# Cosine attention and an x·cos(x) MLP in one kernel: one pipeline over units of six heads instead of two phases

## The chip, the cores and the metric

The kernel runs on one core of one Trainium2 chip. The metric is device time in microseconds (us). Each kernel runs several times, always beside runs of the kernel before on the same chip. The runs were made on more than one chip, so kernels are best compared by their ratios. In these kernels TensorE does the matmuls and transposes, VectorE elementwise work and reductions, ScalarE activations and copies, GpSimd (POOL in the profile) further elementwise work, and SyncE (SP) issues DMA transfers. SBUF is the core's on-chip memory; the rows of a tensor in it are called partitions (64x448 lies on 64 of them). "Unit" means six heads of one batch (16 units), "pair" two heads, and a "step" is a quarter of a pair's scores (12 steps per unit).

## The reference

```python
# q, k, v: (8 batches, 12 heads, 448 tokens, 64); tau = 0.1
q_n = q / (norm(q) + 1e-6);  k_n = k / (norm(k) + 1e-6)
attn = softmax(q_n @ k_n.T / tau)
x = (attn @ v) as (3584 tokens, 768)
h = x @ w_in                    # 768 x 2048
out = (h * cos(h)) @ w_out      # 2048 x 768
```

## The kernel before

It has two blocks, one after the other. The first does attention head by head and writes `xT`; the second does the MLP over tiles of 512 tokens. V is padded with 64 columns of ones, so the product of the exponentials and V holds the softmax sums already repeated on 64 partitions. VectorE takes a reciprocal of all of them, for each of the 96 heads:

```python
def norm(g):                                   # VectorE, once per head
    vec.wait_ge(s_av, g + 1)
    vec.reciprocal(rtmp[gp].ap()[D:2*D, :], AV[gp].ap()[D:2*D, :])   # 64 x 448
    ...
    vec.tensor_tensor(xt_dst, AV[gp].ap()[0:D, :], rtmp[gp].ap()[D:2*D, :], ALU.mult)

for g in range(NG):                            # TensorE
    emit_av(g)                                 # 4 matmuls, 128 columns of V|ones
    if g + 1 < NG: emit_sc(g + 1)              # 4 matmuls, 64 rows each
    if g + 3 < NG: emit_tp(g + 3)              # 8 transposes
# ... a second block: m1 (x @ w_in), Sin on ScalarE, product on VectorE, m2 (@ w_out)
```

## Time and profile before

| | before |
|---|---|
| median time | 841.01 us (840.73 to 841.48, 3 runs) |
| attention | 0 to 522 us |
| MLP | 522 to 838 us |

First, the costliest groups on the page of the kernel before. The columns are: line, engine, operation, tiles, shapes and count; then busy time in us and the mean ns of one; then the engine's idle time just before them and who ended it.

```profile
L237 DVE RECIPROCAL rtmp<-AV 64x448 f32<-64x448 f32 x96 | 284.2, 2960 | 44.1 <-PE AV L352 39.8
L337 PE MATMUL SCP<-qkT_sb 64*112 64x448 bf16 x384 | 166.8, 587 | 56.3 <-DVE qkT_sb L228 54.2
L425 PE MATMUL PH<-xT,W 128*128 128x512 bf16 x672 | 156.5, 383 | 14.7 <-DVE gT L486 10.8
L440 PE MATMUL PO<-W,gT 128*128 128x384 bf16 x896 | 146.6, 326 | 0.0
```

Second, the table of windows of the kernel before: stretch, its length, then busy us (instructions) of TensorE, its weight loads, VectorE, ScalarE and GpSimd, then the granted clock, the DMA share and GB/s. One window lies in attention, one in the MLP.

```profile
200.00:300.00 100.00, 81.67 (x312) 35.37 (x310) 90.68 (x66) 59.33 (x69) 25.52 (x12) 1.00 0.29 72
571.00:592.00 21.00, 21.00 (x130) 12.62 (x129) 0.69 (x1) 3.12 (x4) 0.00 (x0) 1.00 0.19 57
```

In attention VectorE is busy for 91% of the time, and the reciprocal is most of that. In the second window TensorE does almost nothing but second-layer matmuls (128 of 130), one per 0.162 us.

Third, the timeline of TensorE in attention (start us, length us, then the instructions). The weight load of each next score matmul starts with that matmul:

```profile
300.46 1.74 PE L337 MATMUL SCP<-qkT_sb 64*112 64x448 bf16 x4
300.88 0.21 PEld L337 LDWEIGHTS SCP<-qkT_sb 64*112 64x112 bf16 x1 [0.16 <-issue]
301.25 0.21 PEld L337 LDWEIGHTS SCP<-qkT_sb 64*112 64x112 bf16 x1 [0.16 <-issue]
```

The 448 columns take 0.37 us, 1.2 columns per ns, while 384 columns in the MLP take 0.162 us, 2.4 per ns. In the kernel after, whose clock records cover such stretches, first-layer matmuls of 448 columns lie 0.373 us apart at a granted clock of 0.50 and 0.189 us at 1.00 (medians); "half clock" and "full clock" below mean these two rates. In the MLP's first 3.4 us here the matmuls of 512 columns lie 0.427 us apart, and 0.216 us from 525.5 us on. What brings full clock this trace does not show: attention kept TensorE busy for 82% (200 to 300 us) and stayed at half clock to its end, while the MLP, whose waits for VectorE are at most 0.3 us, stayed at full clock from 525.5 us on. The clock column says 1.00 in attention too, only because the trace's first clock record is that of 525.5 us.

### The profile page before, as it was taken

To read this page: it belongs to the slowest core of one execution; us is meant where nothing else is said; L and a number is where in the kernel's file an instruction comes from. 1 tells how busy PE (TensorE), PEld (TensorE's weight loads), DVE (VectorE), ACT (ScalarE), POOL (GpSimd) and SP (SyncE) were. 2 spreads that over 40 slices of the span, in tenths; PEclk is the share of its full clock that TensorE was granted. 3 is DMA by queue.
4 is the path that set the end of the run, shared out by engine and by line. 5 is a ranking of instruction groups with operands and counts; after the bars stand their busy time and mean duration, and the time that the engine had idled before them with its cause. 6 is when DMAs were issued, how large, how long until landed. Compare 5 with 4: busy or idle time off the path is not lost. (4 is left out here: it accounts for less than half of the span.)

```text
span 838.7 us, 7918 instructions
## 1 busy us (share of the span) xinstructions
PE 706.1 (84%) x3104; PEld 321.0 (38%) x3104; DVE 535.0 (64%) x438; ACT 407.3 (49%) x494; POOL 132.1 (16%) x60
## 2 busy tenths in 40 slices
PE   0797797797797797797797797999999999999997
PEld 0343243243243243243333342335454444445464
DVE  3698898898898898898898898441312223131400
ACT  4656656656656656756755733442323333232311
POOL 3434124124113113213213200000000000000000
PEclk9999999999999999999999999999999999999999
DMA  9761452364033043034040000001111020102022
GB/s 286 209 198 61 115 174 80 94 174 89 10 100 99 1 98 97 3 98 98 2 99 0 1 0 1 1 0 39 38 37 39 20 56 20 57 1 76 0 76 76
DMA packets 40516, 57.13 MB, mean 68 GB/s; under 512 B 1824, under 2 KB 34080, under 8 KB 39712
## 3 DMA queue, kind: packets, MB, share of 16 engines
q1 hardware_dynamic: 40480, 56.63, 24.5%
q8 instruction: 25, 0.41, 0.2%
q14 instruction: 11, 0.09, 0.0%
HBM read 45.61 MB, written 11.01 MB: 68 GB/s over the span
## 5 line engine op out<-in xcount | busy, mean ns | idle before, releaser
L237 DVE RECIPROCAL rtmp<-AV 64x448 f32<-64x448 f32 x96 | 284.2, 2960 | 44.1 <-PE AV L352 39.8
L290 ACT ACTIVATE expT<-SCP 112x896 bf16<-112x896 f32 x192 | 165.4, 913 | 165.4 <-PE SCP L337 165.4
L337 PE MATMUL SCP<-qkT_sb 64*112 64x448 bf16 x384 | 166.8, 587 | 56.3 <-DVE qkT_sb L228 54.2
L486 DVE TENSOR_TENSOR gT<-PH,cosh 128x512 bf16<-128x512 f32 x112 | 77.5, 692 | 194.7 <-ACT cosh L459 194.7
L352 PE MATMUL AV<-expT,vp 112*128 112x448 bf16 x384 | 160.5, 572 | 35.4 <-ACT expT L290 34.3
L425 PE MATMUL PH<-xT,W 128*128 128x512 bf16 x672 | 156.5, 383 | 14.7 <-DVE gT L486 10.8
L440 PE MATMUL PO<-W,gT 128*128 128x384 bf16 x896 | 146.6, 326 | 0.0
L337 PEld LDWEIGHTS SCP<-qkT_sb 64*112 64x112 bf16 x384 | 65.7, 200 | 161.1 <-DVE qkT_sb L228 118.6
L459 ACT ACTIVATE cosh<-PH,cst 128x512 f32<-128x512 f32 x112 | 77.0, 688 | 88.3 <-PE PH L425 88.3
L440 PEld LDWEIGHTS PO<-W,gT 128*128 128x128 bf16 x896 | 87.7, 98 | 58.6
L425 PEld LDWEIGHTS PH<-xT,W 128*128 128x128 bf16 x672 | 58.2, 98 | 112.0 <-DVE gT L486 51.0
L177 POOL TENSOR_TENSOR kb<-Kf,rk 112x1536 bf16<-112x1536 f32 x16 | 44.2, 2762 | 340.9 <-ACT rk L281 340.9
L468 ACT ACTIVATE out_sb<-PO 128x768 f32<-128x768 f32 x28 | 22.7, 811 | 123.6 <-PE PO L440 123.6
L352 PEld LDWEIGHTS AV<-expT,vp 112*128 112x128 bf16 x384 | 38.4, 126 | 97.6 <-issue 55.2
L319 PE MATMUL TP<-ident,qs 112*64 112x112 bf16 x384 | 55.7, 301 | 21.7 <-POOL qs L180 21.6
L319 PEld LDWEIGHTS TP<-ident,qs 112*64 112x64 bf16 x384 | 35.3, 158 | 83.6 <-issue 83.6
L228 DVE COPY qkT_sb<-TP 64x896 bf16<-64x896 bf16 x96 | 58.7, 612 | 12.7 <-PE TP L323 11.1
L241 DVE TENSOR_TENSOR xT<-AV,rtmp 64x448 bf16<-64x448 f32 x96 | 59.3, 618 | 3.3
L323 PE MATMUL TP<-ident,kb 112*64 112x112 bf16 x384 | 55.8, 301 | 0.0
L180 POOL TENSOR_TENSOR qs<-Qf,rq 112x1536 bf16<-112x1536 f32 x16 | 44.2, 2762 | 0.0
L323 PEld LDWEIGHTS TP<-ident,kb 112*64 112x64 bf16 x384 | 43.9, 177 | 0.0
L273 ACT ACT_TABLE_LOAD x16 | 20.5, 1283 | 37.8 <-DVE qn L215 37.8
(25 smaller groups left out, 233.5 us busy)
## 6 DMA issues: line engine op xcount, KB each, us to landing
Qf<-in_q_dram SPq DMA_DIRECT2D x16, 672.0 KB, 5.5
Kf<-in_k_dram SPq DMA_DIRECT2D x16, 672.0 KB, 8.5
Vf<-in_v_dram SPq DMA_DIRECT2D x16, 672.0 KB, 9.9
wstage<-in_moe_w_in_dram SPq DMA_DIRECT2D x6, 1024.0 KB, 8.3
wstage<-in_moe_w_out_dram SPq DMA_DIRECT2D x4, 1536.0 KB, 6.7
out_dram<-out_sb SPq DMA_DIRECT2D x8, 336.0 KB, 2.6
out_dram<-out_sb SPq DMA_DIRECT2D x8, 288.0 KB, 2.6
out_dram<-out_sb SPq DMA_DIRECT2D x8, 240.0 KB, 2.5
```

Of the source, the lines that this page charges most:

```text
L228: vec.tensor_copy(qkT_sb[gp].ap(), TP[gp].ap()).then_inc(s_ev, 1)
L237: vec.reciprocal(rtmp[gp].ap()[D : 2 * D, :], AV[gp].ap()[D : 2 * D, :]).then_inc(s_vself, 1)
L241: vec.tensor_tensor(xt_dst, AV[gp].ap()[0:D, :], rtmp[gp].ap()[D : 2 * D, :], ALU.mult).then_inc(s_dv, 1)
L290: act.activation(dst, src, ACT.Exp).then_inc(s_exp, 1)
L319: last = pe.transpose(TP[gp].ap()[0:D, NP * j : NP * (j + 1)], qs[i].ap()[:, col : col + D], ident.ap())
L323: last = pe.transpose(TP[gp].ap()[0:D, S + NP * j : S + NP * (j + 1)], kb[i].ap()[:, col : col + D], ident.ap())
L337: ins = pe.matmul(outap, lhsT, rhs, start=True, stop=True)
L352: ins = pe.matmul(AV[gp].ap(), lhsT, rhs, start=(j == 0), stop=(j == NJ - 1))
L425: ins = pe.matmul(PH[t % 2].ap(), W1v[:, c, 128 * nb : 128 * nb + 128], xTv[:, c, MB * sb : MB * sb + MB], start=(c == 0), stop=(c == NKC ...
L440: ins = pe.matmul(PO[T2 % 2].ap()[:, 512 * n2h : 512 * n2h + N2W], gTv[sbp % 2][:, f, 128 * ms : 128 * ms + 128], W2v[:, f, N2W * n2h : N2 ...
L459: act.activation(cosh[t % 2].ap(), PH[t % 2].ap(), ACT.Sin, bias=cst.ap()[:, 1:2], scale=1.0).then_inc(s_cos, 1)
L486: vec.tensor_tensor(gTv[sb % 2][:, nb, :], PH[t % 2].ap(), cosh[t % 2].ap(), ALU.mult).then_inc(s_gm, 1)
```

## The change

The new kernel keeps one pipeline. Its aims are to get the 96 reciprocals off VectorE, to run the scores of two heads side by side in the two halves of the array, and to fill TensorE's gaps in attention with matmuls of the second MLP layer of earlier batches.

- V gets one column of ones, not 64, so the sums of a head are one row (partition 64 of `xu`).
- Small transfers (`sums`, one per pair) gather the rows of six heads on partitions 0 to 5. One reciprocal (6 x 448) serves six heads. Six transfers, below called the broadcast, then repeat each head's row on 64 partitions (`RB`), and VectorE multiplies.
- First-layer blocks follow every second unit; second-layer matmuls are spread over the steps of units 3 to 15 (`m2_fill`).

The core of the diff, cut (`...`):

```diff
-    vec.reciprocal(rtmp[gp].ap()[D : 2 * D, :], AV[gp].ap()[D : 2 * D, :])      # x96
-    vec.tensor_tensor(xt_dst, AV[gp].ap()[0:D, :], rtmp[gp].ap()[D : 2 * D, :], ALU.mult)
+    def av_tail(g): ...
+        P.op("ACT", lambda e: e.activation(xuv[i][:, 2*p : 2*p+2, :], AVv[0 : D+1, :, 0:S], ACT.Copy, bias=0.0), ...)
+        P.op("SP", lambda e: e.dma_start(sums[i].ap()[2*p : 2*p+2, :], xuv[i][D : D+1, 2*p : 2*p+2, :]), ...)
+    def recip(u):
+        P.op("DVE", lambda e: e.reciprocal(rcp[i].ap(), sums[i].ap()), ...)       # 6 x 448, x16
+        for h in range(UH):
+            o = P.op("SP", lambda e, h=h: e.dma_start(RBv[:, h, :],
+                     bass.AP(rcp[i], h * S, [[S, 1], [0, D], [1, S]])), ...)      # one row to 64 partitions
+    def normalise(u, a):
+        P.op("DVE", lambda e: e.tensor_tensor(xTv[b % 2][...], xuv[i][0:D, a::2, :], RBv[:, a::2, :], ALU.mult), ...)
...
+    def unit(u, per_quantum):
+        for kq in range(4 * UP):              # 12 steps
+            scores(g, c)                      # two heads, rows 0-63 and 64-127 of the array
...
+            if kq == 6 and u >= 1:  recip(u - 1)
+            if kq >= 10 and u >= 1: normalise(u - 1, kq - 10)
+            if per_quantum: m2_fill(per_quantum[kq % len(per_quantum)])
...
+            if c == 3 and g + 1 < NG: transposes(g + 1)
...
+        if u >= 2 and u % 2 == 0:
+            m1(u // 2 - 1)
```

## The prediction

> **What bounds the kernel now.** It has two phases in series. The table of windows puts attention at 0 to 522 us and the MLP at 522 to 838 us. In attention VectorE is busy 0.91 (200 to 300 us): per head a reciprocal of 2.96 us, a copy of 0.61 and a multiply of 0.62, so 4.19 us x 96 heads = 402 us, plus reductions. TensorE hides under it, but barely, because it runs at half speed: by the timeline, starts of its 448-column matmuls lie 0.37 us apart[...]; in the MLP 512 columns take 0.216 us from 525.5 us on. The clock row shows 1.0 throughout. [...]the MLP's first 3.4 us have 0.427 us per matmul. The MLP is TensorE-bound: 672 x 0.216 + 896 x 0.1625 = 291 us.
>
> **What the change does.**
> - Reciprocals: 96 x 2.96 = 284 us become 16 of the same length (448 elements on 6 partitions): 47 us.
> - The sums become one row: AV has 65 columns, its copy goes to ScalarE (48 x 0.91 us).
> - The second layer (896 matmuls) is spread over units 3 to 15, the first layer stays in eight dense blocks. The bound moves to TensorE.
>
> **New load of TensorE, full clock.** First layer 768 x 0.189 = 145 us; second 146; score pairs 48 x 4 x 0.19 = 36 if the two row tiles run together (I assume so; no trace shows it); AV 48 x 7 x 0.19 = 64; transposes 48 x 7 x 0.056 = 19. Sum 410 us.
> VectorE about 275 us and ScalarE about 300 us (192 x 0.8 exps, 64 x 1.0 sines, 48 x 0.9 copies, rest) fit below.
>
> **Lost time on TensorE's chain (estimates from this trace).**
> - Switches between row-tiled and full matmuls: 0.13 us now between scores and transposes; 27 per unit, about 0.12 each: 3.2 us a unit.
> - The transposes of a pair are followed at once by its scores: copy 0.61 plus two latencies, 1.1 us, 3 per unit.
> - Units 0 to 2 have no second-layer work and should run at half clock as attention does now: about 22 us each.
>
> Sum: start 14; units 0 to 2, 66; units 3 to 15, 7 x 21.7 + 6 x 24.3 = 298; eight first-layer blocks 145; their entries and exits 8 x 3 = 24; tail (last normalisation, 144 second-layer matmuls, store) 32. **About 580 us, range 500 to 680.** Chances: faster 0.97, same 0.02, slower 0.01.
>
> **What would show each step.**
> - Second-layer matmuls 0.1625 us apart in units 3 to 15; the chain mostly TensorE; units of 22 to 24 us.
> - Paired scores starting within some 10 ns of one another; 0.19 us apart would add 36 us.
> - "PE scores waits for DVE qkT copy", 48 times, about 1 us each.
>
> **What would make it wrong.** The largest risk is the clock: if the half speed returns in units 3 to 15 (their matmuls fill only some 65% of the time), each unit costs up to 12 us more, and the time is 650 to 720 us. If switches cost nothing and copies hide, 500 us. VectorE's order (reciprocal of 2.96 us or a reduction in front of the copy of the transposes) could lengthen each pair's gap by 1 to 2 us, 50 to 100 us in all.

That units 3 to 15 would run at full clock was an estimate of mine.

## The result, and the profile after

| | before | after |
|---|---|---|
| median time | 840.87 us (4 runs) | 927.19 us (925.85 to 927.68, 4 runs) |
| ratio | | 1.1027 (95%: 1.1011 to 1.1042): slower |
| TensorE busy | 706.1 us | 503.7 us |
| VectorE busy | 535.0 us | 276.8 us |
| mean granted clock | (not recorded in attention) | 0.797 |

A ratio is the mean time of one kernel's runs over that of the other's of the same rounds, so it is not quite the ratio of the medians.

The busy times fell as meant and no engine is near full, yet the time rose. The page of the kernel after, busy time and share of the span by engine:

```profile
PE 503.7 (54%) x2768; PEld 237.4 (26%) x2768; DVE 276.8 (30%) x268; ACT 288.4 (31%) x358; POOL 189.9 (21%) x160
```

The chain that ended last, by engine and then by line, names what the time is made of:

```profile
PE 33%; DMA 26%; SPq 21%; DVE 14%; ACT 2%; issue 2%; POOL 2%; ACTq 0%
DMA RB<-rcp 24%; SPq L379 19%; PE SC L401 12%; PE PO L446 8%; PE AV L401 6%; DVE rcp L376 5%; DVE xT L386 5%; PE AV L357 2%; PE SC L339 2%; DMA sums<-xu 2%; PE SC L446 1%; DVE qkT L326 1%; DVE osb L454 1%; ACT xu L369 1%; SPq L262 1%
```

The transfers that repeat the reciprocals (`RB<-rcp`) and their issue (line 379) are 43% of the chain. Groups and DMA issues of the page, the latter with KB each and us from issue to landing:

```profile
L376 DVE RECIPROCAL rcp<-sums 6x448 f32<-6x448 f32 x16 | 47.0, 2936 | 20.5 <-DMA sums<-xu 20.5
L386 DVE TENSOR_TENSOR xT<-xu,RB 64x1344 bf16<-64x1344 f32 x32 | 49.6, 1551 | 350.6 <-DMA RB<-rcp 350.4
RB<-rcp SPq DMA_DIRECT2D x96, 112.0 KB, 13.6
```

The reciprocals cost 47 us, as predicted. VectorE then stands idle for 350 us, in front of the multiply that needs `RB`. The list of waits (who waited for what; us in total, times, longest) shows how this goes on to TensorE:

```profile
DVE xT L386 <- DMA RB<-rcp: 350.4, 16, 24.4
PE SC L339 <- DVE qkT L326: 199.6, 40, 23.0
PE SC L401 <- DVE xT L386: 98.1, 5, 24.0
PE AV L401 <- DVE xT L386: 65.1, 3, 28.1
```

In this trace VectorE took its instructions in the order of the program. Behind the blocked multiply stands the copy of the next pair's transposes (`qkT`): in the timeline below the transposes run at 332.16 us, and their copy starts at 351.90 us, after the multiply, which waited until 348.28 us. So TensorE waits for that copy at the end of half of the units, and for `xT` itself in front of the eight first-layer blocks. The timeline of the kernel after around one such wait, where the brackets hold the engine's idle time and what ended it:

```profile
320.55 2.93 DVE L376 RECIPROCAL rcp<-sums 6x448 f32<-6x448 f32 x1
323.51 15.16 SPq L379 DMA_DIRECT2D RB<-rcp  x6
332.16 0.55 PE L323 MATMUL TP<-ident,qks 128*128 128x128 bf16 x7
338.71 6.76 SPq L371 DMA_DIRECT2D sums<-xu  x2
348.28 3.12 DVE L386 TENSOR_TENSOR xT<-xu,RB 64x1344 bf16<-64x1344 f32 x2 [21.05 <-DMA RB<-rcp]
351.54 0.90 PE L401 MATMUL SC<-xT,W 128*128 128x448 bf16 x2 [18.83 <-DVE xT L386]
351.90 0.62 DVE L326 COPY qkT<-TP 128x896 bf16<-128x896 bf16 x1
```

From the end of the reciprocal (323.5 us) to the multiply (348.3 us) pass 24.8 us, and this is so in all 16 units (24.7 to 25.6 us). Even the issue of the six transfers takes 15 us. The sums of later heads, which go through the same queue, are issued after them.

In the trace's packet records, a packet of 1792 bytes (one row) from `rcp` takes 0.93 us in the median; packets of 1536 bytes of other transfers take 0.13 us. The records of one unit come in rounds of 16, one round each 1.054 us: 16 x 1792 B / 1.054 us = 27.2 GB/s. The 64 packets of one transfer, about 16 in flight at a time, all read one row. My guess, which no trace had shown and which the experiments test, is that the place they read limits the rate. (The word "ports" in two names of runs comes from that guess.)

### The profile page after: what moved, and what is told of

Same layout as the page of the kernel before. It is cut to its first block, busy times and chain, and to the rows that moved or that the text cites. A ratio compares the mean times of both kernels' runs of the same rounds, so it can differ in the third digit from the quotient of the medians. Undisturbed runs are those within 1.5% of the kernel's fastest.

```text
span 924.9 us, 6907 instructions
## 1 busy us (share of the span) xinstructions
PE 503.7 (54%) x2768; PEld 237.4 (26%) x2768; DVE 276.8 (30%) x268; ACT 288.4 (31%) x358; POOL 189.9 (21%) x160
## 4 chain that ended last, share of the span: by engine, by line
PE 33%; DMA 26%; SPq 21%; DVE 14%; ACT 2%; issue 2%; POOL 2%; ACTq 0%
DMA RB<-rcp 24%; SPq L379 19%; PE SC L401 12%; PE PO L446 8%; PE AV L401 6%; DVE rcp L376 5%; DVE xT L386 5%; PE AV L357 2%; PE SC L339 2%; DMA sums<-xu 2%; PE SC L446 1%; DVE qkT L326 1%; DVE osb L454 1%; ACT xu L369 1%; SPq L262 1%
## 5 line engine op out<-in xcount | busy, mean ns | idle before, releaser
L347 ACT ACTIVATE PX<-SC 128x896 bf16<-128x896 f32 x144 | 130.4, 915 | 273.4 <-PE SC L339 271.9
L339 PE MATMUL SC<-qkT 64*128 64x448 bf16 x288 | 56.6, 398 | 212.9 <-DVE qkT L326 199.6
L290 POOL TENSOR_TENSOR sq<-raw 128x896 bf16<-128x896 f32 x47 | 78.2, 1681 | 444.5 <-DVE n L291 433.3
L401 PE MATMUL SC<-xT,W 128*128 128x448 bf16 x516 | 111.9, 377 | 98.1 <-DVE xT L386 98.1
L386 DVE TENSOR_TENSOR xT<-xu,RB 64x1344 bf16<-64x1344 f32 x32 | 49.6, 1551 | 350.6 <-DMA RB<-rcp 350.4
L307 POOL TENSOR_TENSOR qks<-raw,rn 128x896 bf16<-128x896 f32 x47 | 79.3, 1687 | 113.1 <-ACT rn L301 113.1
L401 PE MATMUL AV<-xT,W 128*128 128x448 bf16 x252 | 57.7, 384 | 65.1 <-DVE xT L386 65.1
L401 PEld LDWEIGHTS SC<-xT,W 128*128 128x128 bf16 x516 | 53.0, 103 | 153.1 <-issue 112.1
L357 PE MATMUL AV<-PX,va 128*65 128x448 bf16 x288 | 76.9, 380 | 0.0
L291 DVE TENSOR_REDUCE n<-sq 128x14 f32<-128x896 bf16 x48 | 50.8, 1081 | 36.0 <-POOL sq L290 32.0
L376 DVE RECIPROCAL rcp<-sums 6x448 f32<-6x448 f32 x16 | 47.0, 2936 | 20.5 <-DMA sums<-xu 20.5
L326 DVE COPY qkT<-TP 128x896 bf16<-128x896 bf16 x48 | 29.6, 616 | 29.3 <-PE TP L323 29.3
```

The source lines that it names most:

```text
L290: P.op("POOL", lambda e: e.tensor_tensor(sq[j].ap(), src, src, ALU.mult), [("raw", i, p)], [("sq", j)])
L307: P.op(eng, lambda e: e.tensor_tensor(qksv[i][:, :, h, :].rearrange("p s h d -> p h s d"), rawv[i][:, h, :, :], bass.AP(rn[i], p * 2 * NS, ...
L339: P.op("PE", lambda e, r=r, a=a, rhs=rhs: e.matmul(sc[:, a, 0:S], qkT[j].ap()[r, S + TL + 128 * c : S + TL + 128 * c + 128], rhs, start=Tr ...
L347: P.op("ACT", lambda e: e.activation(PXm[j][:, c], sc[:, :, 0:S], ACT.Exp, scale=1.0 / TAU), ["SC%d" % z], [("PX", j, c)])
L357: P.op("PE", lambda e, c=c: e.matmul(AVv[0 : D + 1, a, 0:S], vav[i][:, 8 * p + 4 * a + c, :], PXm[j][:, c, a, :], start=(c == 0), stop=False),
L376: P.op("DVE", lambda e: e.reciprocal(rcp[i].ap(), sums[i].ap()), [("sums", i, p) for p in range(UP)], [("rcp", i)])
```

## The experiments

The theories: **A**, the place in SBUF that all packets of the broadcast read limits it, and its time goes through VectorE's order to TensorE. **B**, the six issues or the number of packets limit it, wherever they read. **C**, the half clock (mean 0.797) is the loss, and the waits are not. All ratios are to the kernel before in the same rounds. The diffs are shortened: bookkeeping and the calls after the last unit are left out.

### x1_ports: the same broadcast from eight rows, four partitions apart

The `sums` transfers now write eight copies of a head's row, four partitions apart; the reciprocal runs on 64 partitions (2.94 us, as before); each broadcast reads all eight copies.

```diff
-    sums = sbs("sums", 2, [UH, S], F32);  rcp = sbs("rcp", 2, [UH, S], F32)
+    NR, NCP, CST = 64, 8, 4;  HP = [0, 1, 2, 3, 32, 33]
+    sums = sbs("sums", 2, [NR, S], F32);  rcp = sbs("rcp", 2, [NR, S], F32)      # set to 1.0 once
-    dma_start(sums[i].ap()[2*p : 2*p+2, :], xuv[i][D : D+1, 2*p : 2*p+2, :])
+    for h in (2*p, 2*p + 1):
+        dma_start(bass.AP(sums[i], HP[h]*S, [[CST*S, NCP], [1, S]]),
+                  bass.AP(xu[i], D*UH*S + h*S, [[UH*S, 1], [0, NCP], [1, S]]))
-    bass.AP(rcp[i], h * S, [[S, 1], [0, D], [1, S]])
+    bass.AP(rcp[i], HP[h] * S, [[CST * S, NCP], [0, D // NCP], [1, S]])
```

> Only the rows that the broadcast of the reciprocals reads are moved: eight copies of each head's row lie four partitions apart[...]; same bytes, same six transfers to RB per unit (and 12 small sums transfers per pair of units more). Theory A[...]: the six transfers land within about 6 us instead of 25, packets of 1792 bytes take about 0.1 to 0.2 us instead of 0.93, VectorE's wait for RB falls from 350 us to under 60, and the time falls to 600 to 680 us. Theory B (the six issues and the number of packets): the set still takes over 15 us and the time stays over 850 us. Theory C (half clock of TensorE is the loss by itself, the broadcast hides): time stays over 850 us.

Measured: 632.75 us (631.68 to 635.19), ratio 0.7532 (0.7513 to 0.7552), correct. From the reciprocal's end to the multiply now pass 6.6 to 7.3 us instead of 25, and the median packet takes 0.081 us. The six transfers of the last unit, whose packet records stand alone, ran at 152 GB/s instead of 29.6. The wait and the timeline, in the profile of x1_ports:

```profile
DVE xT L395 <- DMA RB<-rcp: 66.9, 16, 6.2
```

```profile
297.81 2.94 DVE L385 RECIPROCAL rcp<-sums 64x448 f32<-64x448 f32 x1 [1.78 <-DMA sums<-xu]
300.79 3.96 SPq L388 DMA_DIRECT2D RB<-rcp  x6
307.42 3.54 DVE L395 TENSOR_TENSOR xT<-xu,RB 64x1344 bf16<-64x1344 f32 x2 [4.31 <-DMA RB<-rcp]
```

The same six issues now take 4 us instead of 15: one issue takes 0.6 us, where in after it took 2.6 us in the median and 4.2 us at most. So most of their length was the queue waiting for the transfers, not a cost of issuing. The time saved, 294 us, is close to 16 units times the 18 us that each transfer became shorter, 290 us. VectorE's wait for `RB` fell by about as much, 284 us. B and C both expected over 850 us.

### x4_twoports: the same edit with neighbouring partitions

x1_ports changed more than the place: there are copies, more `sums` transfers and a reciprocal over more partitions. This control keeps all of that and moves only the partitions. Its expected figures halve the 25 us of after; that neighbouring partitions would give half was a guess.

```diff
-    NR, NCP, CST = 64, 8, 4;  HP = [0, 1, 2, 3, 32, 33]
+    NR, NCP, CST = 48, 8, 1;  HP = [0, 8, 16, 24, 32, 40]
```

> As x1_ports, with the eight copies of a row on eight neighbouring partitions[...]. [...]about 2 us per transfer and 12 to 14 us for the six, VectorE's wait for RB between 100 and 220 us, time between x1_ports and after (about 720 to 800 us). If the limit were that all packets read the very same row (partition), this would be as fast as x1_ports.

Measured: 701.56 us (2 runs), ratio 0.8344 (0.8328 to 0.8361), correct. Wait for `RB`:

```profile
DVE xT L395 <- DMA RB<-rcp: 125.9, 16, 9.8
```

The wait is in the expected range and the time is between x1_ports and after. Both runs read eight rows per transfer, each as often. So where the rows lie decides, and not that all packets read the very same row. What it is about the place was not shown: a transfer reads one row in after (29.6 GB/s in the last unit's packet records), eight neighbouring rows here (79 GB/s) and eight rows four partitions apart in x1_ports (152 GB/s). The time is below my 720 to 800 us: from the reciprocal to the multiply pass 10.4 us, less than the 12 to 14 us that I gave the six transfers alone. Why they are faster was not shown.

### x2_halfcols: half the bytes from the same place

The result is wrong: the other half of `RB` stays at a constant of 0.001.

```diff
-    dma_start(RBv[:, h, :],          bass.AP(rcp[i], h * S, [[S, 1], [0, D], [1, S]]))
+    dma_start(RBv[:, h, 0 : S // 2], bass.AP(rcp[i], h * S, [[S, 1], [0, D], [1, S // 2]]))
```

> Wrong result on purpose: the broadcast copies half the columns of each row from the same place; packets and issues keep their number, bytes are halved. Theory A: the six transfers take about 12.6 us instead of 25, packets 0.47 us, and the time falls by 16 x about 12 us = 150 to 200 us, to 730 to 780 us. Theory B: no change (over 900 us).

Measured: 725.34 us (2 runs), ratio 0.8627 (0.8610 to 0.8644), a little below the expected 730 to 780 us. From the reciprocal to the multiply: 12.1 to 12.9 us, half of 25; median packet 0.406 us; 32 GB/s.

```profile
DVE xT L387 <- DMA RB<-rcp: 148.0, 16, 11.9
```

The number of issues and packets is that of after. The time goes with the bytes, so B falls. The time and VectorE's wait for `RB` both fell by 202 us; in x4_twoports they fell by 226 and 225 us.

### x5_late: the multiply of even units later in VectorE's order

```diff
-            if kq >= 10 and u >= 1:                normalise(u - 1, kq - 10)
+            if kq >= 10 and u >= 1 and u % 2 == 0: normalise(u - 1, kq - 10)
+            if kq in (4, 5) and u >= 2 and u % 2 == 0: normalise(u - 2, kq - 4)
```

> Transfers unchanged, but the multiply by RB of every even unit is issued on VectorE a whole half unit later (steps 4 and 5 of the next unit but one), where its wait should long be over. If VectorE's place in its strict order hands the transfer's time to everything behind it (copies of the transposes, then TensorE): half of the 16 waits vanish, VectorE's wait for RB falls to about 175 us and the time falls by 120 to 170 us, to 760 to 810 us. If the transfers slow other work down directly (loads, sums), the time stays near 927.

Measured: 874.65 us (2 runs), ratio 1.0403 (1.0382 to 1.0424), correct; a gain of 52 us where I expected 120 to 170.

```profile
DVE xT L386 <- DMA RB<-rcp: 256.4, 16, 24.5
```

The direction is right: the transfers were as slow as in after (24.7 to 25.7 us), and a place further back in VectorE's order alone returned time. The size was wrong because ten steps last less than the transfer: most of the moved waits shrank from about 21 to about 8 us and did not vanish. Only 52 of the 94 us of wait came back as time; where the rest went was not settled.

### w1_warm: the half clock by itself

The kernel after has its array at half clock for 377 of 925 us, by the trace's clock records. This run keeps the broadcast slow and the array busy.

```diff
+        if u >= 3:                       # at the end of each unit
+            for x in range(125):
+                P.op("PE", lambda e: e.matmul(AVv[:, 0, 0:HW], W1v[:, 0, 0:128], W1v[:, 1, 0:HW],
+                                              start=True, stop=True), ["W1"], ["AV"])
```

> The kernel after, unchanged but for 125 second-layer-sized dummy matmuls (results never read) at the end of each unit from 3 on, where TensorE idles for the broadcast anyway; about 20 us of them per unit at full clock. The clock record should then show full speed in most of units 3 to 15. Theory A (the transfer's time is what is lost, the half clock is its consequence and mostly falls into idle time): time between 900 and 945 us. Theory C (the half clock is a loss of its own): time below 880 us.

Measured: 918.57 us (911.16 to 921.81), ratio 1.0908 (1.0858 to 1.0959), correct. The table of windows, one row of after and then one of w1_warm (columns as above; the last but two is the granted clock):

```profile
100.00:900.00 800.00, 456.45 (x2505) 215.57 (x2506) 249.16 (x237) 261.60 (x317) 147.50 (x115) 0.80 0.51 55
```

```profile
100.00:900.00 800.00, 705.26 (x4227) 375.61 (x4228) 252.61 (x244) 261.74 (x317) 147.64 (x115) 0.96 0.52 57
```

The clock rose from 0.80 to 0.96 and the time fell by about 1%. That is a net figure, because the 1625 dummies last a little longer than the waits that they fill (the group on the page of w1_warm):

```profile
L512 PE MATMUL AV<-W 128*128 128x384 bf16 x1625 | 266.2, 326 | 0.0
```

In each of the 13 units the last dummy ends 0.3 to 2.2 us after VectorE has released TensorE, about 14 us in all. So the half clock by itself is worth some 1 to 3% (an estimate: 9 us measured, and up to about 14 us that the dummies hid), far from the 294 us of x1_ports. C falls as the main cause. With TensorE busy for 705 instead of 456 of the 800 us most of the half clock went, so it was mostly a consequence of the idle time; with x1_ports it shrinks by itself, to 89 us.

### y1_late, y2_tp, y3_both: the waits that are left in x1_ports

With 67 us of wait for `RB` left, y1 defers the multiply to the next unit and puts each first-layer block, with the second-layer matmuls that follow it, inside that unit; y2 issues each pair's transposes one step earlier; y3 does both.

```diff
# y1_late, on x1_ports
-            if kq >= 10 and u >= 1:      normalise(u - 1, kq - 10)
+            if kq in (1, 2) and u >= 2:  normalise(u - 2, kq - 1)
+            if kq == 3 and u >= 3 and u % 2 == 1:  m1((u - 3) // 2)     # and no longer after even units
# y2_tp, on x1_ports
-            if c == 3 and g + 1 < NG: transposes(g + 1)
+            if c == 2 and g + 1 < NG: transposes(g + 1)
```

> x1_ports with the multiply by RB deferred to steps 1 and 2 of the next unit and each first-layer block to after step 3 of it, so that reciprocal, six issues and transfer (about 10 us) have 7 steps to pass. VectorE's wait for RB (67 us in x1_ports) should fall below 15 us; time 560 to 600 us. If the rest of the time is TensorE's own work, no change from 632.

> x1_ports with each pair's transposes one step (of four) earlier, so that their copy runs beside a step of scores instead of in front of the next scores. The prediction gave this gap about 1.1 us x 48; 16 of them hide behind the wait for RB, so 25 to 40 us less: 592 to 610 us. If the gap costs nothing, 632.

> y1_late and y2_tp together: with both waits gone the units should be set by TensorE, about 19 to 21 us each, time 520 to 560 us. If both edits remove the same idle time, no better than y1_late.

| run | median us | ratio (95%) |
|---|---|---|
| y1_late | 613.85 | 0.7298 (0.7276 to 0.7320) |
| y2_tp | 633.95 | 0.7543 (0.7520 to 0.7566) |
| y3_both | 602.28 | 0.7168 (0.7148 to 0.7189) |

All three are correct. In y1_late VectorE no longer waits for `RB` except in the last unit (the multiply on its page):

```profile
L395 DVE TENSOR_TENSOR xT<-xu,RB 64x1344 bf16<-64x1344 f32 x32 | 55.2, 1724 | 6.5 <-DMA RB<-rcp 6.3
```

Yet only 19 us came back, not 32 to 72. y2_tp alone gave nothing: its wait for `RB` rose instead,

```profile
DVE xT L395 <- DMA RB<-rcp: 78.0, 16, 6.1
```

so what TensorE saved at the transposes it seems to have spent at the next broadcast. Without that wait (y3 against y1) the same edit is worth about 12 us. y3_both (and y5_w2late below, which is no different within the noise) is the fastest kernel, 239 us under the one before. It missed my 520 to 560 us; between 150 and 550 us its TensorE is busy for 89% of the time:

```profile
150.00:550.00 400.00, 357.69 (x2073) 169.30 (x2072) 205.77 (x194) 212.84 (x258) 122.74 (x96) 0.97 0.34 96
```

Part of what it still loses is at the start: units 0 and 1 take 29 and 37 us, against 22 to 24 us for a later unit without a first-layer block.

### z1_dense: what the spreading of the second layer is worth

```diff
# on x1_ports; four result banks from the start
         m2_add(b)
+        m2_fill(10 ** 6)                  # the whole batch's second layer, at once
-            fills = (4,) if b % 2 == 0 else (6, 5, 5)
+            fills = None
```

> x1_ports with the second layer not spread: each batch's second layer runs as one dense block right after its first layer, with four result banks; units hold attention only. If spreading hides work in waits of the units (as the change means it to): units 3 to 15 fall back to about the 22 us and the half clock of units 0 to 2 while the second layer adds 146 us of its own, time 660 to 710 us. If spreading is worth nothing because TensorE has the same work anyway: 632 or below.

Measured: 755.09 us (753.05 to 758.79), ratio 0.8987 (0.8960 to 0.9014), correct. Spreading is worth 122 us on top of x1_ports, more than I expected. Units without second-layer work take 25 to 27 us, about as long as units with it in x1_ports (23 to 29 us), and the mean clock falls from 0.931 to 0.844: in the dense form nothing fills the waits of attention. VectorE's wait for `RB` even rises, from 67 to 100 us.

### y5_w2late: the crowded start

```diff
# on y3_both
-        if u == 0:
+        if u == 1:
             for x in range(4):            # load of w_out, cast on the way
```

> y3_both with the load of the second layer's weights (6.3 MB read) issued one unit later. In y3_both units 0 and 1 take 29 and 37 us and VectorE waits 16 us once for the sums, while the DMA engines are full with weights and inputs. If that crowding is the cause: unit 1 falls to about 22 us, time 580 to 592 us. If not, 600 to 604.

Measured: 601.23 us (596.58 to 604.37), ratio 0.7155 (0.7109 to 0.7202), correct: no clear gain over y3_both. Unit 1 fell from 37 to 21 us as expected, but unit 2 rose from 20 to 35 us, and the first first-layer block began at 104.9 instead of 104.7 us. The load was moved and the long unit moved with it. What would shorten the start is open.

## Why the prediction was wrong

I predicted 580 us with a range of 500 to 680 and got 927. Point by point:

- **What bounded the kernel before, and the half clock in attention**: nothing in the runs speaks against it.
- **Reciprocals 284 to 47 us; loads of VectorE and ScalarE**: right (47.0 us; VectorE 276.8 us against "about 275", ScalarE 288.4 against "about 300"). TensorE's 410 us at full clock can't be read off in one number: it was busy for 503.7 us, part of it at half clock.
- **Row tiles run together**: right. In the trace, the two matmuls of a pair start 4 ns apart in the median, at most 29.
- **Switches of 0.12 us**: about right. At full clock a second-layer matmul starts 0.30 us after the score pair before it (median of 141), of which 0.19 is the stream of 448 columns: 0.11 us. In the kernel before, from scores to transposes at half clock, it was 0.13 us.
- **Blocks of 18 us**: 19.6 to 21.0 us in after, as each starts at a granted clock of 0.50, after TensorE stood idle for 18 to 28 us, and spends 2.6 to 5.4 us at it; 18.3 us in six of the eight in x1_ports.
- **"The largest risk is the clock"**: the half clock did come back in units 3 to 15, but by itself it was worth some 1 to 3% (w1_warm).
- **The step that failed** is the list "Lost time on TensorE's chain" and its sum. It has no term for the way of the sums: gather, reciprocal, and above all the six transfers that repeat six rows on 64 partitions. I counted the reciprocals that the change removes and not the transfer that takes the repetition's place. Measured, that term is 25 us per unit, for which VectorE waits 350 us in all. So "the bound moves to TensorE" failed too: TensorE is 33% of the chain that ended last, the broadcast with its issue 43%, and units of 3 to 15 without a first-layer block take 40 to 47 us, not 22 to 24. I did name VectorE's order as a risk, but with a reciprocal or a reduction of 1 to 2 us in front of the copy; what stood there was a multiply that waits 21 us for a transfer. The term could have been named from the program: 384 rows x 1792 B = 688 KB per unit, which at the 27.2 GB/s measured in after is about 25 us. No trace that I had then showed that rate, so its size could not have been read off. With the term taken down (x1_ports), the same design takes 633 us, inside my range.
- **The 53 us between x1_ports and 580** are smaller misses: the first block of the first layer starts at 103 us, where my terms give about 83 (the 12.6 MB of weights and the first inputs fill the DMA engines then, with a DMA share of 0.87 to 1.09 from 25 to 100 us in after; that this is the cause was not shown), and VectorE still waits 67 us for `RB`. "1.1 us x 48" for the transposes' gap was too much as a saving: the edit that removes it gained nothing alone and about 12 us once `RB` no longer held VectorE up.

## What to carry to other kernels

Before you trade arithmetic for a transfer inside SBUF, multiply out its bytes and ask where the rows of its source lie: a row that is repeated on 64 partitions was read in 64 packets here, and the packets of such a transfer got 27 to 30 GB/s together. Copies of the source four partitions apart made this one nearly four times faster (6.6 to 7.3 us from the reciprocal to the multiply instead of 25); they cost three more small transfers per unit, and VectorE's wait for the sums rose from 20.5 to 31.3 us in all. An operation that waited 21 us for a transfer held up all that stood behind it in VectorE's order, so put it where the transfer has surely ended; and when the busy time of every engine falls but the time does not, look in the chain of waits for what is on no engine.
